# A limit of four weight loads in flight, and a first piece of split chunks, in an attention-then-experts kernel

## The chip, the cores and the metric

The kernel runs on one core of one Trainium2 chip. The metric is the device time of one execution in microseconds (us), the median of several runs. Times inside an execution are read from a hardware profile of one execution, and count from the start of its span.

## The reference

Attention over 8 batches of 12 heads (448 positions, head size 64, causal), whose output is the input of a layer of eight experts. Each token goes to the expert with its highest gate logit; each expert keeps the 80 tokens of highest gate weight; the rest of the output is zero.

```python
scores = scale * np.matmul(q, k.transpose(0, 1, 3, 2))
scores = np.where(mask, -1000000000.0, scores)
attn = np.exp(scores - np.max(scores, axis=-1, keepdims=True))
attn = attn / (np.sum(attn, axis=-1, keepdims=True) + 1e-09)
x = np.matmul(attn, v)                      # to 3584 tokens x 768
...
logits = x @ w_gate                         # 768 x 8
expert_idx = np.argmax(logits, axis=1)
for e in range(E):                          # 8 experts, capacity 80
    ...
    h = np.maximum(x[tok_idx] @ w1[e], 0.0)              # 768 x 1024
    out[tok_idx] = gate_w[tok_idx, None] * (h @ w2[e])   # 1024 x 768
```

## The kernel before, in words

The attention stage comes first, then a short stage that chooses the tokens of each expert, then the experts. The change touches the experts alone, from about 327 us on.

**Chunks and pieces.** A layer of an expert is a matrix `w1[e]` or `w2[e]`, cut into chunks of 128 rows: six chunks of 128x1024 for layer 1, eight of 128x768 for layer 2. A buffer named `wraw` is 3072 columns wide and holds one *piece*: three chunks of layer 1 or four of layer 2. There are 11 such buffers, filled before the expert stage begins with the first 11 entries of the list `PIECES`; the other 21 pieces (74 chunks, one DMA for each) are loaded during the stage by SP's queue, 0.38 MB or 0.5 MB a load, into buffers that have come free.

**What is done with a chunk.** Most chunks are *split*: ScalarE (ACT) makes the f16 high part `wh` (`high`, L1203), VectorE (DVE) the f16 low part `wl` (`low`, L1209), and TensorE (PE) multiplies three times in f16 for each block of 128 columns (L1504 to L1506). A split chunk's part of the buffer is free once its `wl` is made. Seven chunks are *whole*: PE multiplies them in f32 straight from `wraw` (L1501), and their part is free only when that product is done. The order of a layer's products stands in `ORDER`; where a layer has a whole chunk, that comes first (5, 0, 1, 2, 3, 4 for the first layer). Three half layers (`SOONER`) were split long before.

**What sets the order.** `plan_experts` plays through the stage with a table of costs and returns one list of turns: loads (`ld`), splits (`hi`, `lo`), products (`p`), the small steps between layers, and for each load which buffer takes it. The loop at the end of the kernel emits the instructions in that order. Each engine then runs its own instructions in order, and semaphores hold back what isn't ready. There are 12 `wh` and 11 `wl` buffers, so ACT and DVE can be that many chunks ahead of PE.

**How loads wait.** SP issues its DMAs in order. Their landings are told by eight semaphores (DMAHW0 to DMAHW7), which are dealt out in turn. So a load that takes a semaphore again waits until the DMA eight places ahead has landed, and also until the part of the buffer that it overwrites is free.

In `split_ahead`, buffers 3 and 4 are filled with the two pieces of layer 1 of expert 0: chunks 5, 0, 1 and chunks 2, 3, 4. Chunk 5 is a whole one.

Of the kernel before, what the change touches and what calls it, by code (L numbers as in the profile page):

```python
# [50 lines left out]
COST = {"hi1": 950, "hi2": 735, "lo1": 1135, "lo2": 870, "xw": 210, "xh": 460, "xl": 575, "hw": 120, "hh": 330, "hl": 400,  # L51
        "yt": 470, "yo": 490, "xtp": 420, "ytp": 660, "warm": 600, "split": 108, "whole": 224, "ld": 460, "far": 2100, "seen": 100, "slack": 900}
BEGIN = {"ACT": 400, "SP": 1500, "DVE": 5900, "PE": 9400}
GATHERED, GATHERS = [9400, 12500, 14500], 6000


def plan_experts(E, layers, blocks, order, whole, early, pieces, loaded, buffers, his, los, ready_h, ready_l):
# [63 lines left out]
    queue["SP"] = []  # L121
    busy, times, ends, out, gathers = dict(BEGIN), set(BEGIN.values()), {}, [], len(GATHERED)

# [53 lines left out]
def attention_then_moe(  # L177
# [12 lines left out]
    nc = tc.nc  # L190
# [67 lines left out]
    OFF, at = {}, 0  # L258
# [48 lines left out]
    def whole(e, which, c):  # L307

        return c == (NC1, NC2)[which - 1] - 1 and ((e, which) in WHOLE if AHEAD else e < E - which % 2 - 1)
# [3 lines left out]
    ORDER, sooner, PIECES = {}, [], []  # L313
    for x, (e, which) in enumerate(LAYERS):
        cs = sorted(range((NC1, NC2)[which - 1]), key=lambda c: (not whole(e, which, c), c))
        k = (K1, K2)[which - 1]
        if x in AHEAD:
            sooner.append((e, which, cs[:k]))
            PIECES.append((e, which, cs[k:]))
            cs = [c for both in zip(cs[:k], cs[k:]) for c in both]  # L320
        else:
            PIECES += [(e, which, cs[i:i + k]) for i in range(0, len(cs), k)]
        ORDER[e, which] = cs
    SOONER = [(e, which, c) for e, which, cs in sooner for c in cs]
    PIECES = sooner + PIECES
# [17 lines left out]
    def chunk_of(t, k, j):  # L343
        return t[:, j * (PW // k):(j + 1) * (PW // k)]

    def load_chunk(t, e, which, cs, j, x=0, parts=1):
        w = PW // len(cs) // parts
        nc.sync.dma_start(chunk_of(t, len(cs), j)[:, x * w:(x + 1) * w],
                          (w1 if which == 1 else w2)[e, :, cs[j], x * w:(x + 1) * w])

    def load_piece():

# [8 lines left out]
    def split_ahead():  # L361

        if not AHEAD:
            return [], []
        made = [wpool.tile([P, PW], F32, name="wraw", tag="w", bufs=WBUF) for _ in range(WBUF)]
        stage = made[-1]
        loads, splits = [], []
        for m, (e, which, c) in enumerate(SOONER):
            i, j = place_of[e, which, c]
            w = PW // len(PIECES[i][2])  # L370
            raw = stage[:, m % K2 * D:m % K2 * D + w]
            both = chunk_of(made[i], len(PIECES[i][2]), j).bitcast(F16)
            hi, lo = hi_of[e, which, c], lo_of[e, which, c] = both[:, 0:w], both[:, w:2 * w]
            h = w // 2
            loads.append([lambda x=x, raw=raw, e=e, which=which, c=c, h=h: nc.sync.dma_start(
                raw[:, x * h:(x + 1) * h], (w1 if which == 1 else w2)[e, :, c, x * h:(x + 1) * h]) for x in range(2)])
            splits.append([lambda raw=raw: nc.gpsimd.tensor_scalar(raw, raw, SW, None, op0=ALU.mult),
                           lambda hi=hi, raw=raw: nc.gpsimd.tensor_copy(hi, raw)] + [
                lambda a=a, hi=hi, lo=lo, raw=raw, h=h: nc.gpsimd.tensor_tensor(
                    out=lo[:, a:a + h], in0=raw[:, a:a + h], in1=hi[:, a:a + h], op=ALU.subtract) for a in (0, h)])  # L380
        wload.extend(made)
        later = [[lambda t=made[i], p=PIECES[i], j=j, x=x: load_chunk(t, *p, j, x, 2) for j in range(len(PIECES[i][2]))
                  for x in range(2)] for i in range(len(AHEAD), WBUF)]
        loads.append(later.pop())
        parts.extend(f for fs in later for f in fs)
        return loads, splits

    def piece_parts():

        got = []  # L390
        k = len(PIECES[len(wload)][2])
        got.append(piece())
        return [lambda j=j, x=x: load_chunk(*got[0], j, x, 2) for j in range(k) for x in range(2)]
# [806 lines left out]
    def high(y):  # L1200
        src = source(y)
        hi_of[y] = split_bufs["hi"].pop(0)
        nc.scalar.activation(hi_of[y][:, 0:src.shape[1]], src, AF.Copy, scale=SW)  # L1203

    def low(y):
        src = source(y)
        lo_of[y] = split_bufs["lo"].pop(0)
        n = src.shape[1]
        nc.vector.scalar_tensor_tensor(out=lo_of[y][:, 0:n], in0=src, scalar=SW, in1=hi_of[y][:, 0:n], op0=ALU.mult,  # L1209
                                       op1=ALU.subtract)  # L1210
# [160 lines left out]
    for i, x in enumerate(ROW_ENGINES):  # L1371
        g, t = divmod(i, NT)
# [38 lines left out]
    def gather(u):  # L1411
        e, s = u.e, u.s
        sn = min(SL, CAP - s * SL)
        u.sn = sn
        u.rows = max(2, sn)
        u.xg = xg_bufs[e % len(xg_bufs)]
        nc.gpsimd.indirect_dma_start(
            out=u.xg[0:u.rows, :], out_offset=None, in_=xs[:, :],
            in_offset=bass.IndirectOffsetOnAxis(ap=idx[s][0:u.rows, e:e + 1], axis=0),
            bounds_check=N - 1, oob_is_err=False)  # L1420
# [133 lines left out]
    for s in range(NSL):  # L1554
        units = [Unit(e, s) for e in range(E)]
        if s:
            for made in (raw_of, hi_of, lo_of):
                made.clear()
            del wload[BUFS:]
        turns = plan_experts(E, LAYERS, (None, NF, NC1), ORDER, whole, [] if s else SOONER, PIECES, 0 if s else BUFS, BUFS, HIS, LOS,  # L1560
                             0 if s else 3, 0 if s else 2)
        bufs = wload[0:BUFS]
        for u in units[:len(GATHERED)]:
            gather(u)
            if u.e == 0:
                nc.gpsimd.memset(split_bufs["lo"][0][:, 0:1], 0.0)  # L1566
        token_weights[s]()
        gathered = len(GATHERED)
        for (kind, e, *y), info in turns:
            u = units[e]  # L1570
            if kind == "hi":
                high((e, *y))
            elif kind == "lo":
                low((e, *y))
            elif kind == "ld":
                b, i, j = info
                load_chunk(bufs[b], *PIECES[i], j)
                raw_of[(e, *y)] = chunk_of(bufs[b], len(PIECES[i][2]), j)
            elif kind == "p":
                (u.last_layer if e == E - 1 and y[0] == 2 else u.product)(*(y[1:] if e == E - 1 and y[0] == 2 else y))  # L1580
                if not whole(e, *y) and (s or (e, *y) not in SOONER):
                    split_bufs["hi"].append(hi_of[(e, *y)])
                    split_bufs["lo"].append(lo_of[(e, *y)])
            elif kind == "warm":
                if PER == NC1:
                    warm = ps_m.tile([P, PER * SL], F32, name="wp", tag="misc")
                    for _ in range(3):
                        nc.tensor.matmul(warm, identb, before[:, 0:PER * SL], start=True, stop=True)
            else:
                getattr(u, kind)()  # L1590
                if kind == "xtp" and gathered < E:
                    gather(units[gathered])
                    gathered += 1
        units[-1].ytp()
        units[-1].yo()
# [44 lines left out]
```

## Time and profile before

| what | value |
|---|---|
| median of 3 runs | 446.72 us (446.46 to 448.32) |
| the profiled execution's own time | 446.64 us |
| its span | 444.6 us |
| PE busy, of the span | 419.5 us (94%) |
| DVE, ACT, POOL busy | 379.3, 388.3, 286.9 us |
| granted TensorE clock in every stretch of the expert stage | 1.00 |
| weight loads of the expert stage | 74, issued from 327.05 to 413.8 us |

The span is the time from the first to the last instruction of the profile; 2.0 us of the execution's own time lie around it. Busy time is a mean over stages, so the expert stage has to be read by itself. PE's matmuls and weight loads into the array (PEld) are separate instructions of one sequence.

### The profile page before, as it was taken

The page shows a single profiled execution, that of the slowest core. Times are in us where ns is not written, and L with a number is a line of the kernel's source. Part 1 is how long each engine was busy: PE and PEld are TensorE (multiplying, and loading weights), DVE is VectorE, ACT ScalarE, POOL GpSimd, SP SyncE. Part 2 cuts the span into 40 slices and gives each one's busy share as a digit, 9 for nine tenths or more (in the row PEclk, how much of TensorE's full clock was granted, in tenths as well). Part 3 has the DMA queues.
Part 4 walks back from the last instruction along what each step waited for, and adds up shares of the span by engine and source line. Part 5 has one row for each costly group of instructions (what it writes and reads, how often), then busy time and mean ns, then how long its engine had stood idle before and what let it go on. Part 6 is the DMA issues. An engine that isn't in the chain of part 4 may idle for free.

```text
span 444.6 us, 15877 instructions
## 1 busy us (share of the span) xinstructions
PE 419.5 (94%) x5847; PEld 325.2 (73%) x5847; DVE 379.3 (85%) x1302; ACT 388.3 (87%) x1062; POOL 286.9 (65%) x439
## 2 busy tenths in 40 slices
PE   7899999999999999999999999999789999888894
PEld 3666777677777777767777777766469999887893
DVE  6777788979889898988998989888879999989791
ACT  5899999999989999998999998978868979878891
POOL 7967998998898898899889885412462242210021
PEclk9899999999999999999999999999999999999999
DMA  7485668859786974976664387199359999999701
GB/s 224 147 272 184 195 227 285 291 201 295 241 282 199 290 242 152 297 253 212 214 215 144 124 243 272 66 349 312 126 171 349 403 403 411 393 414 413 306 27 46
DMA packets 49869, 109.95 MB, mean 247 GB/s; under 512 B 5970, under 2 KB 27474, under 8 KB 49152
## 3 DMA queue, kind: packets, MB, share of 16 engines
q1 hardware_dynamic: 48592, 105.20, 68.4%
q0 software_dynamic: 1056, 3.51, 2.4%
q8 instruction: 46, 0.75, 0.7%
q14 instruction: 31, 0.25, 0.2%
q10 hardware_dynamic: 144, 0.23, 0.2%
HBM read 85.35 MB, written 23.99 MB: 246 GB/s over the span
## 4 chain that ended last, share of the span: by engine, by line
PE 83%; ACT 5%; DVE 4%; issue 3%; POOL 2%; DMA 1%; POOLq 0%; DVEq 0%; ACTq 0%
PE xp L662 18%; PE tp L638 17%; PE sp L580 12%; PE rt L773 4%; ACT prob L603 4%; PE hp L1505 3%; PE hp L1506 3%; PE hp L1504 3%; PE op L1504 3%; PE op L1506 3%; PE op L1505 3%; PE gp L723 3%; PE sp L587 2%; PE hp L1501 2%; PE wp L1370 1%
## 5 line engine op out<-in xcount | busy, mean ns | idle before, releaser
L603 ACT ACTIVATE prob<-ns,nb 128x192 f32<-128x192 f32 (+3 forms) x336 | 175.5, 532 | 14.6 <-DVE nb L599 13.1
L599 DVE CUSTOM_DVE_ANT_0 ns<-sp,mask 128x192 f32<-128x192 f32 (+3 forms) x336 | 134.5, 443 | 17.7 <-PE sp L580 16.5
L638 PE MATMUL tp<-ident,prob 128*128 128x128 f32 x768 | 105.9, 279 | 0.1
L528 POOL TENSOR_TENSOR qk<-qk,qk 128x448 f16<-128x448 f32 x94 | 98.1, 1059 | 4.5 <-DVE qk L556 2.3
L1209 DVE SCALAR_TENSOR_TENSOR wl<-wraw,wh 128x768 f16<-128x768 f32 (+1 forms) x93 | 94.7, 1073 | 5.5 <-POOL wl L1566 2.1
L662 PE MATMUL xp<-PT,vt 128*64 128x448 f32 (+3 forms) x768 | 93.6, 386 | 0.2
L1203 ACT ACTIVATE wh<-wraw 128x768 f16<-128x768 f32 (+1 forms) x93 | 82.1, 941 | 12.3 <-PE hp L1505 5.9
L638 PEld LDWEIGHTS tp<-ident,prob 128*128 128x128 f32 x768 | 85.2, 142 | 3.2 <-ACT PT L643 0.5
L643 ACT COPY PT<-tp 128x512 f32<-128x512 f32 x144 | 77.0, 589 | 8.3 <-PE tp L638 7.0
L662 PEld LDWEIGHTS xp<-PT,vt 128*64 128x64 f32 x768 | 50.9, 136 | 44.7 <-issue 23.3
L580 PE MATMUL sp<-qk 64*128 64x448 f16 (+2 forms) x864 | 68.4, 297 | 2.9 <-POOL qk L528 1.8
L1506 PEld LDWEIGHTS <-wl 128*128 128x128 f16 x644 | 64.3, 100 | 3.9 <-issue 3.9
L603 ACT ACTIVATION_READ_ACCUMULATOR prob<-ns,nb 128x1 f32 x336 | 66.3, 197 | 0.0
L1504 PEld LDWEIGHTS <-wh 128*128 128x128 f16 x644 | 64.6, 100 | 1.7 <-issue 1.6
L1505 PEld LDWEIGHTS <-wh 128*128 128x128 f16 x644 | 64.3, 100 | 0.9 <-issue 0.8
L1550 POOL DMA_INDIRECT out<-yo,idx x8 | 15.6, 1954 | 69.4 <-ACT yo L1547 65.0
L580 PEld LDWEIGHTS <-qk 64*128 64x128 f16 x864 | 36.5, 94 | 17.7 <-issue 2.9
L643 DVE COPY PT<-tp 64x256 f32<-64x256 f32 x144 | 43.6, 328 | 2.9 <-PE tp L638 0.8
L1505 PE MATMUL hp<-xl,wh 128*128 128x80 f16 x344 | 38.8, 202 | 2.1 <-DVE xl L1449 1.2
L1506 PE MATMUL hp<-xh,wl 128*128 128x80 f16 x344 | 38.8, 202 | 1.1 <-issue 1.1
L1504 PE MATMUL hp<-xh,wh 128*128 128x80 f16 x344 | 38.9, 202 | 0.0
L556 POOL CAST qk<-qk 128x896 f16<-128x896 f32 x40 | 36.2, 935 | 0.4
(198 smaller groups left out, 734.7 us busy)
## 6 DMA issues: line engine op xcount, KB each, us to landing
wraw<-w SPq DMA_DIRECT2D x45, 384.0 KB
wraw<-w SPq DMA_DIRECT2D x31, 512.0 KB
out<-mask SPq DMA_DIRECT2D x56, 192.0 KB
qk<-k_t SPq DMA_DIRECT2D x23, 448.0 KB
qk<-q_t SPq DMA_DIRECT2D x23, 448.0 KB
vt<-v_t SPq DMA_DIRECT2D x24, 384.0 KB
xs<-xr SPq DMA_DIRECT2D x42, 192.0 KB
wraw<-w SPq DMA_DIRECT2D x24, 192.0 KB
```

Of the source, the lines that this page charges most:

```text
L528: sub = lambda e, o, a, b: e.tensor_tensor(out=o, in0=a, in1=b, op=ALU.subtract)
L580: nc.tensor.matmul(pr.sp[t, j], a[rows, p, queries(t)], c[rows, p, FROM[t]:FROM[t] + WIDTH[t]], start=(x == 0), stop=(x == 2))
L599: nc.vector.tensor_tensor_reduce(out=ns, in0=pr.sp[x], in1=m, scale=-1.0 / 8.0, scalar=HUGE, op0=ALU.add, op1=ALU.min, accum_out=nb)
L603: nc.scalar.activation(pr.P[:, OFF[x]:OFF[x] + w], got[0], AF.Exp, bias=got[1], scale=-1.0, accum_out=pr.sums[:, h:h + 1])
L638: nc.tensor.transpose(tp[:, i * P:(i + 1) * P], f, ident)
L643: way(part_of(pr.PT, rows, to, *todims), part_of(got[0], rows, at, *dims))
L662: nc.tensor.matmul(xp[rows, to:to + w], st["vt"][:, c, p * P + j * DH:p * P + (j + 1) * DH], pr.PT[:, j, n0:n0 + w], start=(c == 0), stop= ...
L1203: nc.scalar.activation(hi_of[y][:, 0:src.shape[1]], src, AF.Copy, scale=SW)
L1209: nc.vector.scalar_tensor_tensor(out=lo_of[y][:, 0:n], in0=src, scalar=SW, in1=hi_of[y][:, 0:n], op0=ALU.mult, op1=ALU.subtract)
L1504: nc.tensor.matmul(o, wh[:, ws], h[:, c, :], start=begin, stop=False, skip_group_check=True)
L1505: nc.tensor.matmul(o, wh[:, ws], l[:, c, :], start=False, stop=False, skip_group_check=True)
L1506: nc.tensor.matmul(o, wl[:, ws], h[:, c, :], start=False, stop=end, skip_group_check=True)
```

## The change

Two edits. The list `began` keeps the loads in order, and each load from the fifth on gets a wait for the landing of the load four places ahead of it. And the first ordinary layer of the list (layer 1 of expert 0) is cut into pieces in the order of the chunks' numbers, so that buffer 3 holds chunks 0, 1, 2, all of them split, and buffer 4 holds chunks 3, 4, 5. `ORDER`, which sets PE's products, stays.

```diff
+IN_FLIGHT = 4
...
         else:
-            PIECES += [(e, which, cs[i:i + k]) for i in range(0, len(cs), k)]
+            at = cs if PIECES else sorted(cs)
+            PIECES += [(e, which, at[i:i + k]) for i in range(0, len(cs), k)]
         ORDER[e, which] = cs
...
-        nc.sync.dma_start(chunk_of(t, len(cs), j)[:, x * w:(x + 1) * w],
-                          (w1 if which == 1 else w2)[e, :, cs[j], x * w:(x + 1) * w])
+        return nc.sync.dma_start(chunk_of(t, len(cs), j)[:, x * w:(x + 1) * w],
+                                 (w1 if which == 1 else w2)[e, :, cs[j], x * w:(x + 1) * w])
...
+        began = []
         for (kind, e, *y), info in turns:
...
             elif kind == "ld":
                 b, i, j = info
-                load_chunk(bufs[b], *PIECES[i], j)
+                began.append(load_chunk(bufs[b], *PIECES[i], j).ins)
+                if len(began) > IN_FLIGHT:
+                    tc.add_manual_dep(began[-1], began[-1 - IN_FLIGHT].name,
+                                      mybir.DependencyInfo(mybir.DependencyClass.Sync, mybir.DependencyReason.DATA),
+                                      reason="weights in flight")
```

On PE, ACT, DVE and POOL no instruction changes its place; only buffer numbers change. On SP the 74 loads keep their order of chunks; their buffers and waits change.

SP's queue at the start of the expert stage, before: the last write of the token rows (`xs`), then the first nine loads. `wraw_188` is buffer 4 (chunks 2, 3, 4 of expert 0), `wraw_187` is buffer 3 (chunks 5, 0, 1), `wraw_5724` is buffer 6.

```order
L798 DMA xs<-xrl_6563 128x384 [waits DMAHW3_49,Pool_49]
L348 DMA wraw_188<-w2 128x768 [waits DMAHW4_49,DVE_49]
L348 DMA wraw_188<-w2 128x768 [waits DMAHW5_49,DVE_49]
L348 DMA wraw_188<-w2 128x768 [waits DMAHW6_49,DVE_49]
L348 DMA wraw_188<-w2 128x768 [waits DMAHW7_49]
L348 DMA wraw_187<-w1 128x1024 [waits DMAHW0_49,PE_49]
L348 DMA wraw_187<-w1 128x1024 [waits DMAHW1_49]
L348 DMA wraw_187<-w1 128x1024 [waits DMAHW2_49]
L348 DMA wraw_5724<-w1 128x1024 [waits DMAHW3_49,DVE_49,Activation_49]
L348 DMA wraw_5724<-w1 128x1024 [waits DMAHW4_49,DVE_49,Activation_49]
```

The same place on SP in the changed kernel, where `wraw_187` now holds chunks 0, 1, 2 and `wraw_188` chunks 3, 4, 5.

```order
L800 DMA xs<-xrl_6563 128x384 [waits DMAHW3_49,Pool_49]
L350 DMA wraw_187<-w2 128x768 [waits DMAHW4_49,DVE_49]
L350 DMA wraw_187<-w2 128x768 [waits DMAHW5_49,DVE_49]
L350 DMA wraw_187<-w2 128x768 [waits DMAHW6_49,DVE_49]
L350 DMA wraw_187<-w2 128x768 [waits DMAHW7_49]
L350 DMA wraw_188<-w1 128x1024 [waits DMAHW4_49,DMAHW0_49,DVE_49]
L350 DMA wraw_188<-w1 128x1024 [waits DMAHW5_49,DMAHW1_49,DVE_49]
L350 DMA wraw_188<-w1 128x1024 [waits DMAHW6_49,DMAHW2_49,PE_49]
L350 DMA wraw_5724<-w1 128x1024 [waits DMAHW3_49,DMAHW7_49,DVE_49,Activation_49]
L350 DMA wraw_5724<-w1 128x1024 [waits DMAHW0_49,DVE_49,Activation_49]
```

The first four loads go to the buffer of chunks 0, 1, 2, whose `wl` of chunks 0 and 1 are made before the stage. The wait for PE (the product of the whole chunk 5) moves from the fifth load to the seventh. From the fifth load on, the semaphore of the load four places ahead is waited for, and from the ninth on it stands in place of the load's own.

SP's queue in the middle of the stage, before: six loads of layer 1 of expert 5 and two of layer 2 of expert 4.

```order
L348 DMA wraw_188<-w1 128x1024 [waits DMAHW0_49,DVE_49,Activation_49]
L348 DMA wraw_188<-w1 128x1024 [waits DMAHW1_49,DVE_49,Activation_49]
L348 DMA wraw_188<-w1 128x1024 [waits DMAHW2_49,DVE_49,Activation_49]
L348 DMA wraw_5724<-w1 128x1024 [waits DMAHW3_49,DVE_49]
L348 DMA wraw_5724<-w1 128x1024 [waits DMAHW4_49,DVE_49]
```

The same five in the changed kernel.

```order
L350 DMA wraw_187<-w1 128x1024 [waits DMAHW4_49,DVE_49,Activation_49]
L350 DMA wraw_187<-w1 128x1024 [waits DMAHW5_49,DVE_49,Activation_49]
L350 DMA wraw_187<-w1 128x1024 [waits DMAHW6_49,DVE_49,Activation_49]
L350 DMA wraw_5724<-w1 128x1024 [waits DMAHW7_49,DVE_49]
L350 DMA wraw_5724<-w1 128x1024 [waits DMAHW0_49,DVE_49]
```

Here only the semaphore differs: each waits for one that was dealt out four loads ago and not eight.

## Rows read from the trace of the kernel before

**Rows 1.** Windows: length, busy us (instructions) by engine, clock, DMA share, GB/s

```profile
331.00:336.00 5.00, 3.82 (x101) 3.82 (x101) 5.00 (x6) 2.94 (x5) 2.66 (x2) 1.00 1.00 331
344.00:349.00 5.00, 4.62 (x113) 4.49 (x112) 5.00 (x7) 4.67 (x9) 1.77 (x1) 1.00 1.03 411
349.00:384.00 35.00, 33.95 (x759) 33.58 (x756) 33.95 (x39) 31.29 (x47) 9.20 (x6) 1.00 1.03 400
384.00:418.00 34.00, 28.08 (x718) 27.33 (x714) 28.45 (x33) 27.00 (x39) 4.56 (x3) 1.00 1.03 414
418.00:422.00 4.00, 2.92 (x82) 2.79 (x79) 4.00 (x6) 4.00 (x9) 0.00 (x0) 1.00 0.40 157
422.00:434.60 12.60, 12.60 (x333) 12.58 (x330) 12.60 (x16) 11.57 (x19) 2.97 (x2) 1.00 0.09 24
```

**Rows 2.** Waits of PE from 348 to 422: us in total, times, longest

```profile
PE op L1506 <- issue: 3.0, 3, 1.0
PE op L1504 <- issue: 2.5, 3, 1.3
PE ytp L1537 <- issue: 1.1, 1, 1.1
PE hp L1506 <- issue: 1.1, 1, 1.1
PE hp L1505 <- issue: 0.7, 1, 0.7
```

**Rows 3.** Windows cut where PE's idle times end, columns as in the first group

```profile
385.60:391.59 5.99, 4.98 (x128) 4.84 (x127) 4.79 (x7) 3.19 (x5) 0.74 (x1) 1.00 1.02 416
391.59:397.51 5.92, 5.21 (x128) 5.06 (x128) 4.90 (x6) 5.38 (x8) 0.45 (x1) 1.00 1.03 415
...
415.33:421.38 6.05, 4.97 (x128) 4.84 (x127) 4.07 (x7) 4.65 (x9) 0.00 (x0) 1.00 0.72 285
421.38:426.40 5.02, 5.00 (x128) 5.00 (x128) 5.02 (x7) 5.02 (x9) 1.60 (x1) 1.00 0.02 5
426.40:430.99 4.59, 4.59 (x134) 4.59 (x131) 4.59 (x7) 4.59 (x7) 1.26 (x1) 1.00 0.20 57
```

**Rows 4.** DMA from 391.59 to 397.51: packets, MB, share; issues, us to landing

```profile
q8 instruction: 1, 0.02, 1.0%
...
out<-yo,idx POOLq DMA_INDIRECT x1, 6.8
```

**Rows 5.** The same from 430.99 to 436

```profile
q8 instruction: 1, 0.02, 1.2%
...
out<-yo,idx POOLq DMA_INDIRECT x1, 4.2
```

**Rows 6.** Waits of SP's queue from 327 to 414

```profile
SPq L348 <- DMA wraw<-w: 48.8, 60, 1.7
SPq L348 <- DVE wl L1209: 10.5, 13, 5.1
```

**Rows 7.** Timeline of SP: start, us, instruction

```profile
321.32 0.55 SPq L798 DMA_DIRECT2D xs<-xrl  x1
327.05 87.30 SPq L348 DMA_DIRECT2D wraw<-w  x74
```

**Rows 8.** Timeline of DVE from 415 to 438, in brackets the idle time before

```profile
417.33 0.66 DVE L1449 SCALAR_TENSOR_TENSOR xl<-xtp,xh 128x480 f16<-128x480 f32 x1 [1.98 <-ACT xh L1443]
...
427.58 7.03 DVE L1209 SCALAR_TENSOR_TENSOR wl<-wraw,wh 128x768 f16<-128x768 f32 x8
```

**Rows 9.** The chain that ended last, the step after PE's last product

```profile
437.37 0.42 DVE yt L1523
```

**Rows 10.** Timeline of ACT, its last split

```profile
432.01 0.84 ACT L1203 ACTIVATE wh<-wraw 128x768 f16<-128x768 f32 x1
```

**Rows 11.** Timelines of POOL and PE as the stage begins

```profile
324.56 1.08 POOL L1417 DMA_INDIRECT xg<-xs,idx  x1 [5.16 <-DVE gws L1134]
...
322.68 5.46 PE L1370 MATMUL wp<-before,identb 128*128 128x448 bf16 x28
```

## The prediction

> **What bounds the kernel now.** The page says PE is busy for 94% of the span, but that is a mean. The change touches only the expert stage, so I read the stage by windows first [rows 1]. Up to 384 us PE is nearly full (33.95 of 35.00 us). From 384 to 418 it is idle for 34.00 - 28.08 = 5.9 us, from 418 to 422 for 1.1, and after that not at all. The DMA share changes at the same place: 1.03 up to 418, 0.40 in the next four microseconds, 0.09 after them. The granted clock is 1.00 throughout, so the clock has no part in it.
>
> The waits of PE come next [rows 2]. There are nine from 348 to 422, of about a microsecond each, 8.4 us in all, and none is for a buffer, a split or a load: they stand as "issue", so nothing that the profile shows was missing.
>
> Then I cut windows where these idle times end [rows 3]. Each of them holds 128 matmuls and 127 or 128 weight loads: 256 instructions. That regular count is the key. A wait for data would follow layers and chunks; this one comes after every 256th instruction, whatever it is. In two windows of one block each, one with loads and one without (it follows the last of these rows), the queue of kind "instruction" moved one packet of 0.02 MB [rows 4, 5]. So I read the idle time as PE waiting for its next block of instructions, fetched by DMA once a block. While weights stream, a block takes 5.92 to 6.05 us, of which PE works 4.97 to 5.21; as soon as they end, a block of as many instructions takes 5.02 or 4.59 us with no idle time [rows 3]. The fetch, some 5.95 us from block to block, is slower than the work by 0.8 to 1.1 us, and only beside the loads.
>
> One rule speaks against this. The Trainium skill ("Runtime: NRT & Kernel Launch", section "Instruction fetch mechanics") says that instructions come in blocks of 256 over a queue of the engine's own, and that the crossing of a block is mostly hidden. The count of 256 agrees with the trace, the hiding does not: by the page there would be nothing to win, by the rows there are 8.4 us.
>
> **The change part by part.** *The limit of four.* SP's queue waited 60 times for the landing of an earlier load, 48.8 us in all [rows 6]: eight loads were in flight nearly always. The 74 issues take 87.30 us [rows 7], 1.18 each, so a load is issued about 9.4 us after the one eight places ahead, and 4.7 us after the one four ahead. The change therefore takes about 4.7 us of queued weights from in front of whatever else wants the DMA engines. The fetch has to become quicker by 0.8 to 1.1 us for the stalls to go, a fifth of that. How the fetch's wait hangs on the queue no row shows. Its bounds are: no gain at all (0) and all of it (8.4). The nearest rows are those of a scatter, a DMA on another queue too: it landed in 6.8 us beside the loads and in 4.2 without them [rows 4, 5], 2.6 more. Half of that is 1.3, more than the 1.1 that is needed, so I take all of the 8.4 as the likeliest.
>
> *What comes of the 8.4 us.* PE does not keep them all, since DVE is close behind. DVE has no idle time from 417.33 on: it is full in 418 to 422 and in 422 to 434.60 [rows 1], and its last `wl` ends at 427.58 + 7.03 = 434.6 [rows 8]. That run began after 1.98 us of waiting for `xh` of the last expert, which follows PE's transposes, and so PE's stalls. Before it DVE was idle for 34.00 - 28.45 = 5.55 us in the window from 384, the 1.98 among them [rows 1]. If PE loses its stalls, DVE can move up by 5.55 us and no further (another 1.05 us of idle time lies before 384). At the end PE finishes by 437.37 [rows 9], 2.8 us after the last `wl`. In PE's order (`last_layer`) 36 of the 54 matmuls of the last three chunks follow that `wl`: the last chunk's part of the first half, then the whole second half. At 4.59 us for 134 or 5.02 for 128 [rows 3] that is 1.2 to 1.4 us. So the tail can give another 1.4. Together 5.55 + 1.4 = 6.95 us, less than the 8.4. I take 6.0: the waits of DVE for `xh` need PE, ACT and DVE in a row, and I expect about a microsecond of them to stay.
>
> *The price of the limit.* Nothing but loads stands behind the waiting load on SP, so the wait itself holds up no other work. It can only make the weights late. They have room: the last `wh` is made at 432.01 [rows 10], while the last load is issued at about 414 [rows 7] and the DMA share falls between 418 and 422 [rows 1]; I take 421 for its landing. That is 11 us, and 5 us once the stage is 6 us shorter. From 344 on the DMA moved 411 x 5 + 400 x 35 + 414 x 34 + 157 x 4 = 30.8 MB in 77 us [rows 1]. To be done by 426 it needs 376 GB/s, 9% less than 414. The bounds of the rate with four loads: 414, as now, and 331, that of 331 to 336 [rows 1], soon after the first loads began. There the share was 1.00 already, and gathers of token rows ran beside the loads, which is why I take a value near the upper end: a loss of at most a few per cent, which the 11 us hide.
>
> *The first piece.* SP had issued its last row write at 321.32 and was free at 321.87, then waited 5.1 us, its longest wait for DVE, for the first load's part of the buffer [rows 6, 7]. The first two loads now go where `wl` was made before the stage, so they start at about 322, 5 us sooner: 0.79 MB, 1.9 us of transfer at 414 GB/s, off the end of the stream. It is more room, not time, as loads were not waited for. A cost could come from a meeting with the first gather (issued at 324.56), on which PE's first transposes wait; but the two loads need until about 322 + 1.9 and some issue time, and PE is filled by 28 warm-up matmuls to 322.68 + 5.46 = 328.1 anyway [rows 11]. If that cover failed, the stage would begin later by what is left of the two loads, at most 1.9 us. I count 0.
>
> *Sum.* 446.64 (the execution's own time) - 6.0 = 440.6; the median of the runs lies 0.08 above that execution, so 440.7.
>
> **The rivals.** *Half.* The fetch gets quicker, but by half of what is needed. Then 4.2 us of stalls stay, DVE's limit no longer counts, and the time is 446.7 - 4.2 = 442.5, or up to 444.5 where less than half goes. For it: blocks vary from 4.59 to 5.21 us of work, so some may fit and others not.
>
> *The fetch takes turns.* If the fetch's wait is set by how the engines serve several queues and not by how much is queued on one, a shorter queue changes nothing. For it: the scatter landed only 2.6 us later beside the loads [rows 4, 5], though some 9 us of them were queued: it did not stand behind all of them. Against it: all rows are of eight in flight, so none shows the wait at another depth. The stalls would stay, and the time would be 446.7, give or take 1. The Trainium skill ("DMA: Bandwidth & Descriptors", section "Queues, rings and completion order") states such a rule: each DMA engine goes round the queues that have work, a packet at a time. The scatter's row bears it out in part.
>
> *Weights come late.* With four in flight the engines run dry between a landing and the next issue. At 331 GB/s the 30.8 MB would take 93 us, to 437.1, 5.1 us after the last `wh` was made before; the end moves with it, to 446.6 + 5.1 = 451.7. It decides from about 350 GB/s down: there the last landing is at 432 and the gain is gone. Against it: a load has 4.7 us from the issue four places ahead, and share 1.00 was reached early in the stage [rows 1].
>
> **How the numbers follow.** The forecast has 0.62 (439.0 to 442.2 by itself: the DVE sum of 6.95 with some of the 1.05, down to 4.5), half 0.14, turns 0.13, late weights 0.11. A difference within 0.5% (2.2 us) can hardly be told from none here. Faster is the forecast and most of half, 0.74; the same is turns and the rest, 0.15; slower 0.11. The range reaches from 438.6, where nearly all of the 8.4 us are kept, to 446.0, so that it leaves out late weights and much of turns.
>
> **What would show it.** Right: PE's waits marked "issue" between 348 and 422 fall from 8.4 us to under 2, windows of 128 matmuls last about 5 us under load, SP's waits for landings remain, and the DMA rate stays above 376 GB/s. DVE should be nearly full from 384 on. Wrong: the stalls still stand at every 256th instruction (turns), or ACT's `wh` and PE's whole products wait for `wraw` (late weights). If the first step holds and the time still does not fall, DVE's order was tighter than I summed.

## The result, and the profile after

The change made the kernel slower: 452.48 us (median of 4 runs, 450.1 to 453.55) against 446.85 us (4 runs, 446.46 to 448.32), a ratio of 1.0112 with a 95% interval of 1.0066 to 1.0159. The prediction was 440.7 (438.6 to 446.0). The profiled execution took 452.68 us, with a span of 450.8, 6.2 us more than before.

The windows of the changed kernel, columns as in [rows 1], and two more at the end:

```profile
331.00:336.00 5.00, 5.00 (x124) 5.00 (x123) 5.00 (x6) 3.47 (x6) 2.52 (x2) 1.00 1.02 323
344.00:349.00 5.00, 5.00 (x135) 5.00 (x131) 5.00 (x7) 4.67 (x10) 2.16 (x1) 1.00 0.95 303
349.00:384.00 35.00, 33.03 (x732) 32.69 (x732) 33.30 (x37) 29.91 (x45) 13.31 (x5) 1.00 0.97 326
384.00:418.00 34.00, 29.17 (x738) 28.38 (x738) 27.93 (x30) 27.38 (x38) 2.61 (x3) 1.00 0.96 344
418.00:422.00 4.00, 3.29 (x76) 3.09 (x76) 3.80 (x6) 4.00 (x8) 0.00 (x0) 1.00 0.95 334
422.00:434.60 12.60, 9.81 (x256) 9.40 (x254) 11.32 (x15) 9.77 (x15) 0.92 (x1) 0.99 0.98 339
434.60:440.00 5.40, 3.15 (x34) 2.97 (x35) 2.77 (x3) 3.19 (x5) 0.76 (x1) 0.50 0.03 13
440.00:451.00 11.00, 4.41 (x90) 3.89 (x87) 1.02 (x2) 0.95 (x2) 1.07 (x2) 0.81 0.16 46
```

Read the last column first. The DMA moved 326 to 344 GB/s from 349 to 434.6, where it moved 400 to 414 before [rows 1], and the weights, which were all there by 422, now come until 434.6. Read the share beside it: 0.95 to 0.98, near the 1.03 of before. The share alone would not have told that the rate had fallen by a sixth.

The waits of PE from 348 to 451 (us in total, times, longest), which answer to [rows 2]:

```profile
PE ytp L1539 <- ACT yt L1530: 4.5, 1, 4.5
PE hp L1506 <- ACT xh L1445: 2.2, 2, 1.6
PE op L1508 <- issue: 1.8, 2, 1.1
PE op L1506 <- issue: 1.8, 1, 1.8
PE hp L1507 <- DVE xl L1451: 1.0, 2, 0.5
PE op L1508 <- DVE wl L1211: 0.5, 1, 0.5
PE hp L1507 <- issue: 0.4, 2, 0.3
PE ytp L1539 <- DVE yt L1525: 0.2, 1, 0.2
```

What was meant to fall has fallen: "issue" is 1.8 + 1.8 + 0.4 = 4.0 us, from 8.4. But 8.4 us of waits for ACT and DVE stand here, of which before had only the 0.2 at the bottom. So I look at what ACT waits for, from 327 to 440:

```profile
ACT wh L1205 <- DMA wraw<-w: 8.1, 11, 1.3
```

Eleven splits waited for their weights, 8.1 us in all; before there was no such wait. ACT works in order, so what stands behind a late split is late too. At the end of the stage this can be followed, on ACT's timeline (start, us, instruction, in brackets the idle time before and what ended it):

```profile
432.68 1.79 ACT L1205 ACTIVATE wh<-wraw 128x768 f16<-128x768 f32 x2 [1.24 <-DMA wraw<-w]
435.50 0.84 ACT L1205 ACTIVATE wh<-wraw 128x768 f16<-128x768 f32 x1 [1.03 <-DVE wl L1211]
436.24 0.55 ACT L1530 ACTIVATE yt<-op 128x480 f32<-128x480 f32 x1
436.69 0.83 ACT L1205 ACTIVATE wh<-wraw 128x768 f16<-128x768 f32 x1
```

and on PE's and DVE's:

```profile
436.85 1.50 PE L1539 MATMUL ytp<-ident,yt 128*80 128x128 f32 x6 [4.53 <-ACT yt L1530]
```

```profile
437.56 0.96 DVE L1211 SCALAR_TENSOR_TENSOR wl<-wraw,wh 128x768 f16<-128x768 f32 x1 [0.23 <-ACT wh L1205]
443.59 0.41 DVE L1525 TENSOR_SCALAR yt<-hp 128x240 f32<-128x240 f32 x1 [5.07 <-PE hp L1508]
```

`yt` stands in ACT's order behind the late splits, and PE stood 4.53 us for it. The last split began at 436.69, 4.7 us later than before [rows 10], and PE's last product ended by 443.59, 6.2 us later [rows 9]: the whole difference of the spans. The other 1.5 us lie behind that split. There PE had much of its tail still to do, and until 440 it did it at a granted clock of 0.50, that is 1.2 GHz, to which the clock had fallen while PE was without work. How the 1.5 us divide between the two was not measured.

SP's timeline, and from the DMA view of 349 to 418 the loads of which issue and landing could be paired (count, KB each, median us from one to the other):

```profile
321.30 109.59 SPq L350 DMA_DIRECT2D wraw<-w  x74
```

```profile
DMA packets 7109, 23.09 MB, mean 335 GB/s; under 512 B 902, under 2 KB 902, under 8 KB 7094
...
q1 hardware_dynamic: 6583, 21.12, 88.1%
...
wraw<-w SPq DMA_DIRECT2D x24, 512.0 KB, 6.2
wraw<-w SPq DMA_DIRECT2D x22, 384.0 KB, 5.5
```

The first load starts at 321.30 and not at 327.05 [rows 7], as said. But the 74 issues take 109.59 us, so four of them 5.92, and a load needs 5.5 to 6.2 us from issue to landing. I had put 4.7 there, half of the 9.4 us of eight loads.

### The profile page after: what moved, and what is told of

It reads as the page before. It is cut to its first block, busy times and chain, and to the rows that moved or that the text cites. A ratio compares the mean times of both kernels' runs of the same rounds, so it can differ in the third digit from the quotient of the medians.

```text
span 450.8 us, 15879 instructions
## 1 busy us (share of the span) xinstructions
PE 421.4 (93%) x5847; PEld 326.2 (72%) x5847; DVE 379.7 (84%) x1302; ACT 389.1 (86%) x1062; POOL 287.8 (64%) x439
## 4 chain that ended last, share of the span: by engine, by line
PE 81%; DMA 7%; DVE 4%; ACT 3%; POOL 2%; issue 1%; POOLq 0%; ACTq 0%; SPq 0%; DVEq 0%
PE xp L664 19%; PE tp L640 18%; PE sp L582 13%; DMA wraw<-w 6%; PE rt L775 4%; PE gp L725 2%; PE hp L1507 2%; PE hp L1508 2%; PE hp L1506 2%; PE hp L1503 2%; PE sp L589 2%; PE op L1506 2%; PE op L1507 2%; PE op L1508 2%; PE wp L1372 2%
## 5 line engine op out<-in xcount | busy, mean ns | idle before, releaser
L640 PE MATMUL tp<-ident,prob 128*128 128x128 f32 x768 | 104.6, 276 | 0.1
L1205 ACT ACTIVATE wh<-wraw 128x768 f16<-128x768 f32 (+1 forms) x93 | 83.4, 942 | 19.1 <-DMA wraw<-w 8.1
L640 PEld LDWEIGHTS tp<-ident,prob 128*128 128x128 f32 x768 | 83.9, 141 | 3.2 <-ACT PT L645 0.5
L1507 PEld LDWEIGHTS <-wh 128*128 128x128 f16 x644 | 65.0, 101 | 2.9 <-issue 2.7
L1506 PEld LDWEIGHTS <-wh 128*128 128x128 f16 x644 | 65.3, 101 | 1.2 <-issue 1.2
```

The source lines that it names most:

```text
L640: nc.tensor.transpose(tp[:, i * P:(i + 1) * P], f, ident)
L1506: nc.tensor.matmul(o, wh[:, ws], h[:, c, :], start=begin, stop=False, skip_group_check=True)
L1507: nc.tensor.matmul(o, wh[:, ws], l[:, c, :], start=False, stop=False, skip_group_check=True)
```

## The experiments

The theory after the result: the limit does shorten PE's wait for the instruction fetch (for its next block of instructions), but with the bytes of four loads in flight the DMA moves only some 335 GB/s, and the weights end too late. Its rivals: the limit costs something by itself (the added waits, the order on SP); the new first piece is what costs; the stalls were not the loads' doing, so that there was nothing to win.

In one table, all kernels. GB/s are those of the windows 349 to 384 and 384 to 418; "issue" is PE's, from 348 to 422; "wraw" is ACT's wait for loads, from 327 to 440; the last column is how long SP takes to issue all loads. Kernels that ran together share the runs of before: 446.7 us for e1 to e4, 447.65 for e5 to e8, 446.86 for e9 to e11. All but before, e2 and e4 have the new first piece, so what a limit does by itself is read against e1. Times are medians, but each trace is of one execution: those of e3 (447.43 us) and e9 (443.40) were the longest of their kernel, that of e7 (442.36) the shortest.

| kernel | median us (runs) | ratio to before, 95% | GB/s | issue us | wraw us | issues us |
|---|---|---|---|---|---|---|
| before | 446.72 | | 400, 414 | 8.4 | 0 | 87.30 |
| the change | 452.48 (4) | 1.0112, 1.0066 to 1.0159 | 326, 344 | 4.0 | 8.1 | 109.59 |
| e1 first piece only | 445.11 (10) | 0.9969, 0.9952 to 0.9987 | 399, 403 | 6.6 | 0 | 89.77 |
| e2 limit only | 453.72 (4) | 1.0170, 1.0144 to 1.0195 | 338, 350 | 0.2 | 7.7 | 105.51 |
| e3 limit of six | 445.00 (10) | 0.9970, 0.9956 to 0.9984 | 379, 399 | 6.9 | 0 | 94.18 |
| e4 no loads | 437.23 (4) | 0.9791, 0.9760 to 0.9822 | 32, 25 | 0 | 0 | none |
| e5 limit of five | 444.20 (4) | 0.9915, 0.9898 to 0.9931 | 359, 374 | 5.4 | 0 | 100.13 |
| e6 halves by partitions | 482.08 (4) | 1.0765, 1.0747 to 1.0783 | 253, 260 | 10.1 | 17.5 | 141.81 (148 halves) |
| e7 four from the 41st load | 444.52 (5) | 0.9937, 0.9920 to 0.9953 | 382, 355 | 5.4 | 0 | 100.46 |
| e8 four from the 57th load | 443.26 (4) | 0.9895, 0.9875 to 0.9914 | 401, 371 | 4.9 | 0 | 96.45 |
| e9 four, every sixth load left out | 440.85 (4) | 0.9855, 0.9833 to 0.9877 | 321, 337 | 4.2 | 0 | 94.08 (62 loads) |
| e10 halves by columns | 451.65 (4) | 1.0120, 1.0089 to 1.0151 | 342, 346 | 1.7 | 4.3 | 107.92 (148 halves) |
| e11 five, four from the 57th | 444.01 (4) | 0.9926, 0.9909 to 0.9944 | 375, 375 | 5.6 | 0 | 100.96 |

**e1 and e2: each edit alone.** e1 keeps the new first piece and lifts the limit out of reach; e2 keeps the limit and cuts the first piece as before.

```diff
 e1
-IN_FLIGHT = 4
+IN_FLIGHT = 1000
 e2
-            at = cs if PIECES else sorted(cs)
+            at = cs
```

> The first piece of split chunks alone, no limit on loads in flight. If the limit is what costs (the queue of loads too short, weights late): 446 to 447 us, PE's waits marked issue stay near 8.4 us, and the DMA rate from 349 to 418 stays near 400 to 414 GB/s. If the two early loads are what costs, by meeting the first gather or by a slower start: 449 to 452 us, with the first product of the experts later than 329.0 us.

> The limit of four alone, the first piece as before. If the limit costs: 452 to 455 us, a rate near 330 to 345 GB/s from 349 on, ACT waiting about 8 us or more for loads, since the two early loads no longer take 0.79 MB off the stream. If the early loads cost: 446 to 447 us or faster.

The loss is the limit's: 453.72 without the new piece. The new piece gains a little, 0.3%, some 1.4 us, where I had written 446 to 447. The window from 418 to 422 of e1 shows where most of it stands:

```profile
418.00:422.00 4.00, 4.00 (x104) 3.99 (x102) 4.00 (x7) 4.00 (x7) 0.00 (x0) 1.00 0.07 25
```

The loads, begun earlier, are all but done by 418 (25 GB/s here, 157 before), and PE, which was idle for 1.1 us of this window, is full: the last stall of [rows 2], 1.1 us, is gone with the load traffic beside it. In this trace PE's last product ends 1.8 us sooner than before, and most of the other 0.7 lies in two stalls before 361 us that were shorter.

In e2 PE's waits are these, from 348 to 422:

```profile
PE hp L1506 <- ACT xh L1445: 3.9, 3, 1.8
PE hp L1507 <- DVE xl L1451: 1.5, 3, 0.5
PE ytp L1539 <- ACT yt L1530: 1.1, 1, 1.1
PE op L1506 <- issue: 0.2, 1, 0.2
```

Almost no "issue" is left, and yet the kernel is the slowest of those with whole loads. I read it so: an engine that waits for data gives the fetch time to arrive. Then the 0.2 us here are not what the limit would leave of the stalls with the weights in time; e9, which has them in time, has 4.2.

**e4: no loads.** The 74 loads of the expert stage are left out, with the first piece as before; the experts compute with what the buffers hold.

```diff
-                began.append(load_chunk(bufs[b], *PIECES[i], j).ins)
-                if len(began) > IN_FLIGHT:
...
```

> The 74 loads of the expert stage are left out: the products use what the buffers held before, the rest of the work stays. If the stalls at every 256th instruction come from the loads: no wait of PE marked issue over 0.3 us, and the time falls by what I summed, 6 to 7 us, to 439.7 to 441 us. If they are the fetch's own, beside loads or not: stalls stay near 8 us and the time near 446.7.

From 348 to 422 PE has no wait at all, and these are two windows:

```profile
349.00:384.00 35.00, 35.00 (x802) 34.97 (x799) 35.00 (x40) 32.87 (x50) 16.90 (x6) 1.00 0.12 32
384.00:418.00 34.00, 34.00 (x897) 33.97 (x894) 34.00 (x41) 33.12 (x50) 15.22 (x4) 1.00 0.09 25
```

The stalls are the loads' doing, and taking the loads away is worth 446.7 - 437.2 = 9.5 us. That is more than the 8.4 of the stalls, and more than the 6.95 that I took to be the most that DVE allows. (I had written 439.7 to 441.)

That the stalls are waits for the fetch can be read from the single packets in the traces. Every wait marked "issue" of over 0.2 us that PE has from 348 us on, in every kernel, ends at the same place of a block: at instruction 193 of 256, counting PE's matmuls and weight loads from the start. In the kernel before, the 16 KB packet of the queue of kind "instruction" starts 3.5 to 4.0 us after PE has passed such a place (349 to 418 us, mean 3.7), and in its nine stalls PE goes on 2.2 to 2.5 us after that start. Together that is the 5.95 us from block to block. Without loads the packet starts 0.2 us after the place in the mean, 1.3 at most.

**e9: four in flight, fewer bytes.** This tells the late weights from a cost of the limit itself. The limit and its waits stay, but every sixth load is left out, so that the stream is shorter; those chunks are computed from what the buffer held.

```diff
-                began.append(load_chunk(bufs[b], *PIECES[i], j).ins)
+                turned += 1
+                if turned % 6 != 0:
+                    began.append(load_chunk(bufs[b], *PIECES[i], j).ins)
```

> The changed kernel with the limit of four, but every sixth weight load of the expert stage is left out (62 of the 74 remain, each of its full size), so that chunk is computed from what the buffer held before. Late weights: the rate with four in flight stays at 325 to 350 GB/s, but the stream has 16% fewer bytes and ends near 418 instead of 436, before any split waits for it; ACT's waits for wraw go to under 1 us, PE's waits for instructions stay at about 4 us, and the time is 440 to 443 us. The limit costs by itself (the wait on SP's queue, or something else than bytes): the time stays at 449 us or more, although fewer bytes are loaded.

The windows around the end of the stream, and PE's waits from 348 to 422:

```profile
384.00:418.00 34.00, 29.98 (x771) 29.37 (x771) 31.05 (x36) 29.62 (x45) 4.52 (x3) 1.00 0.95 337
418.00:422.00 4.00, 4.00 (x103) 3.99 (x102) 4.00 (x6) 4.00 (x8) 0.51 (x1) 1.00 0.44 169
```

```profile
PE op L1506 <- issue: 1.4, 1, 1.4
PE ytp L1539 <- issue: 1.1, 1, 1.1
PE hp L1508 <- issue: 0.8, 1, 0.8
PE op L1508 <- issue: 0.7, 1, 0.7
PE op L1507 <- issue: 0.2, 1, 0.2
```

The rate is as low as in the changed kernel (337 GB/s), the loads end between 418 and 422, no split waits for one, and the time is 440.85, 6.0 us under before. No cost of the limit but the late weights is seen here. And with the weights in time 4.2 us of stalls stay, of 8.4 before and of 6.6 in e1, which has the first piece alone: the fetch is quicker, but by less than was needed. (The profiled execution, with 443.4 us, was the longest of the four.)

**e10 and e6: what sets the rate.** Each load is made as two DMAs, with at most eight of them in flight: the bytes of four loads, in twice as many transfers. e10 halves the columns, e6 the partitions (two DMAs of 64 partitions each).

```diff
 e10
-                began.append(load_chunk(bufs[b], *PIECES[i], j).ins)
+                for x in range(2):
+                    began.append(load_chunk(bufs[b], *PIECES[i], j, x, 2).ins)
 e6
+                for rows in (slice(0, P // 2), slice(P // 2, P)):
+                    began.append(nc.sync.dma_start(chunk_of(bufs[b], len(pcs), j)[rows],
+                                                   (w1 if pw == 1 else w2)[pe, rows, pcs[j], :]).ins)
```

> Each weight load is made as two DMAs of half its columns, all 128 partitions each, with at most eight halves in flight: the bytes of four loads. Bytes in flight set the rate: 325 to 350 GB/s from 349 to 418, ACT's waits for wraw at 7 us or more, and 449 to 454 us. The number of transfers in flight sets it: 390 to 415 GB/s, as with eight whole loads, waits for wraw under 1 us, and a time at or under that of the kernel before, 443 to 447 us. If the halves are slower to move by themselves, as the halves by partitions were, the rate falls under 325 GB/s and the time passes 455 us.

> Each load cut into two DMAs of 64 partitions, eight halves in flight: as many bytes in flight as four loads, released in finer steps, and packets of the same size. If the bytes in flight set the rate: 335 to 355 GB/s and 450 to 453 us. If it is the wait for a whole load, whose last DMA engine ends some 2 us after its first, the rate rises to 370 GB/s or more and the time falls to 447 us or less.

e10 moves 342 and 346 GB/s, the changed kernel 326 and 344, and takes about as long. Twice as many transfers do not bring the rate back: the bytes in flight set it. One rival is that e10's packets are half as large. They are a little slower for their size: from 349 to 418 the median packet of 2048 B took 84 ns, against 159 ns for 4096 B in the changed kernel, and one of 1536 B took 65 ns, against 121 for 3072 B. These 6 to 7% are too little for 342 in place of 400. ACT's wait was less than I had written, 4.3 us for at least 7. e6, for which I had written 450 to 453 us or less, tells nothing on this, since its halves are slower by themselves: the median packet of 3072 B took 194 ns there. Its windows:

```profile
349.00:384.00 35.00, 30.36 (x615) 29.78 (x613) 25.84 (x31) 24.06 (x36) 5.00 (x5) 0.90 1.04 253
384.00:418.00 34.00, 26.20 (x559) 25.45 (x556) 20.69 (x23) 21.15 (x29) 2.67 (x3) 0.90 1.02 260
```

But it repeats the lesson on the share: 1.04 and 1.02 at 253 and 260 GB/s. The Trainium skill ("SBUF — State Buffer", section "Door 1: The DMA port swizzle (why `[64,N]` ≈ `[32,N]`)") says that 64 partitions reach only 8 of the 16 ports of the memory, and gives 196 GB/s for such a transfer of 1 MiB against 328 for 128 partitions; the fall agrees in kind, and no run here shows the ports.

**e3 and e5: six and five in flight.**

```diff
-IN_FLIGHT = 4
+IN_FLIGHT = 6    (e3)
+IN_FLIGHT = 5    (e5)
```

> Both edits with six loads in flight in place of four. If the rate is set by how much is in flight, six loads (2.6 MB) that land in some 6 us should be near 400 GB/s again, and the weights come in time: then the time tells whether the fetch of instructions gets quicker already. 442 to 445 us if PE's stalls fall to 4 us or less, 446 to 447 if they stay at 8.4. If every load less in flight costs rate (six eighths of 414 is 310): 453 us or more.

> Both edits with five loads in flight. Seen so far from 384 to 418: 344 GB/s at four, 399 at six, 403 to 414 without a limit. If the rate grows with what is in flight: 365 to 380 GB/s, the last landing near 427, and the time between those of six and four, 445 to 448 us. If PE's stalls begin to fall at five already (under 5 us) while the weights still come in time: 441 to 444.

The rate rises with each load in flight (326, 359, 379, 399 GB/s for 4, 5, 6 and 8 from 349 to 384), and the stalls with it: 5.8 us at five and 8.0 at six, with the 0.4 and 1.1 us that lie just behind 422, since the loads end later there. That six has more than the 6.6 of e1, without a limit, shows how far single traces differ. At five nothing waits for a load yet, and the kernel is 0.85% faster than before. The limit of six gains nothing: e3 is as fast as e1.

**e7, e8 and e11: the limit where there is room.** A lower rate costs nothing as long as the weights are ahead. e7 keeps the limit of four from the 41st load on, e8 from the 57th; e11 has five in flight and four from the 57th.

```diff
-                if len(began) > IN_FLIGHT:
+                if len(began) > 40:         (e7)
+                if len(began) > 56:         (e8)
 e11
+                far = 4 if len(began) > 56 else 5
+                if len(began) > far:
```

> First piece of split chunks, and the limit of four only from the 41st load on. Those 34 loads are about 14 MB: at 340 GB/s in place of 405 they take some 41 us, not 35, so the last lands near 426. If the limit is good for the fetch and bad only for the rate, PE's stalls from 384 on fall from 7 us to about 2 to 4 and the weights are just in time: 441 to 444 us. If the fetch does not get quicker at four: 445 us. If the weights are late after all: 446 to 449.

> The same with the limit of four only from the 57th load on, 18 loads, about 7.3 MB: 3.4 us more, the last landing near 423. Stalls of PE after about 397 us (some 5 us of the 8) can shrink, the earlier ones stay: 442 to 444 us if the fetch gets quicker, 445 if not. Weights should not be late in any case.

> The limit is five up to the 56th load of the expert stage and four from the 57th on. If the gain of the limit of five (0.9915 of before) and that of the late limit of four (0.9895) come from different blocks, they add up in part: 441 to 443 us, PE's waits for instructions 4 us or less from 348 to 422. If the rate of five in flight (359 GB/s from 349 to 384) uses up the room that the late limit needs, the last loads come late: ACT waits for wraw for 2 us or more, and the time is 444 to 448 us.

All three beat both kernels. e8 is the best, 443.26 us, 1.05% under before, some 0.7% of it more than e1; its interval meets that of e5. e7, with 444.52, is hardly to be told from e1, whose interval it meets. In e11 the two limits did not add up to the 441 to 443 us of my first case: 444.01, with 5.6 us of "issue", and no split waits for a load, so late weights are not why. Which of its blocks miss the fetch was not followed further.

## Why the prediction was wrong

**The step that failed: the price of the limit.** I took the rate with four loads "near the upper end: a loss of at most a few per cent, which the 11 us hide". It was 335 GB/s (349 to 418), below the 376 that I had said was needed and close to my lower bound of 331. The rival *weights come late* came true: it gave 451.7, and 452.48 was measured. That it came so near is in part luck. The loads had begun earlier, so that their last packet ended at 435.9 and not at 437.1, and the 1.5 us behind the last split, which the rival did not count, made up for it. Two readings led to the wrong price.

The first is the sentence against that rival, "a load has 4.7 us from the issue four places ahead". Halving the queue does not halve the time to a landing. Per group of loads in flight, SP's issues take 89.77 x 8 / 74 = 9.70 us for eight (e1), 7.64 for six, 6.77 for five, 5.92 for four. From eight to four that is 3.78 us, 0.95 a load, so some 5.92 - 4 x 0.95 = 2.1 us of a group don't shrink (an estimate, by a straight line; SP's waits for free buffers are in these times too). The Trainium skill ("DMA: Bandwidth & Descriptors", section "Anatomy of one DMA — SWDGE (gpsimd) path") has such a part: about 2.0 us of each DMA that do not depend on its size, most of it until the last byte is confirmed, and 436 GB/s besides. Its figures are for DMAs issued from another engine; by them four loads of 0.461 MB (the mean of the 46 above) would land in 2.0 + 4 x 0.461 / 0.436 = 6.2 us, an estimate that is near the 5.5 to 6.2 of the trace.

The second is the share of 1.00 beside 331 GB/s in [rows 1], which I read as a full DMA held up by gathers. The share does not tell full from half-idle: it was 0.97 at 326 and 1.04 at 253 GB/s. What it counts is the time that packets take, and that grows in the mean. From 349 to 418 the loads' queue had 6583 packets in 88.1% of 16 engines' 69 us, 148 ns each, and before:

```profile
DMA packets 8932, 28.06 MB, mean 407 GB/s; under 512 B 1103, under 2 KB 1103, under 8 KB 8918
...
q1 hardware_dynamic: 8406, 26.10, 95.2%
```

that is 125 ns each. The usual packet is not slower: the median is 121 ns for 3072 B and 159 ns for 4096 B in both traces. But 8% of the packets took more than one and a half times the median of their size, against 1.2% before; why these take longer stays open. And the engines do run dry in part, as the rival put it: for 38% of these 69 us fewer than 16 packets were under way on the 16 engines, before never. The share does not show it, since the records of some packets overlap.

**The stalls.** Right in kind, wrong in size. They belong to the loads (e4: none without them) and the limit shortens them, but I took all 8.4 us where 4.2 go (e9), and 1.8 of these by the first piece (e1). That is the rival *half*, which gave 442.5; e9, with no late weights, took 440.85. *The fetch takes turns* is wrong as an all or nothing, but the wait is not in proportion to the queue either. From the place of the block to the start of the fetch's packet it took, in the mean from 349 to 418, 3.7 us at eight (before) or 3.5 (e1), 3.5 at six, 3.3 at five, 3.2, 2.8 and 2.6 at four (the changed kernel, e9, e2) and 0.2 without loads. I had taken 1.3 us off, half of what the scatter lost beside the loads; 0.8 to 1.1 were needed, and the mean of e9 is 0.9 below before. So some blocks fit and others don't. A low rate alone does not shorten the wait: in e6, at 253 GB/s, its mean is 4.1.

**What comes of them.** The bound of 6.95 us by DVE was too low: without loads the kernel gained 9.5 us, with DVE full from 349 to 418. I had counted DVE's idle time from 384 on and 1.4 us of tail. DVE's timeline in e4 shows which term was wrong:

```profile
419.51 7.03 DVE L1211 SCALAR_TENSOR_TENSOR wl<-wraw,wh 128x768 f16<-128x768 f32 x8
428.02 0.41 DVE L1525 TENSOR_SCALAR yt<-hp 128x240 f32<-128x240 f32 x1 [1.49 <-PE hp L1508]
```

The tail behind the last `wl` gave 1.3 us (1.49 in place of 2.76), as summed. But the last `wl` ends at 426.54, 8.1 us sooner and not 5.55: the 1.05 us of idle time before 384, which I had left out, went as well. Where the other 1.5 was to be found was not followed further.

**The first piece.** Its loads started 5.75 us earlier, at 321.30, and PE went from the warm-ups to the first transposes without a wait, so the first gather did not suffer. (The transposes began at 328.85, 0.9 us later than before, since the warm-ups took longer; the last section has their clock.) I counted 0; by itself it gains 0.3% (e1), in the main because the loads are gone from beside the last stall. With the limit it cannot be told from nothing (1.0112 and 1.0170, whose intervals meet).

**The room.** The 11 us fit what came: the loads ended some 14 us later than the 421 that I had read (their last 0.29 MB came after 434), and that is more than the room. The engines' order made it worse: `yt` waits on ACT behind a split, and PE behind `yt`.

## What to carry to other kernels

Before a limit is put on transfers in flight, work out the bytes in flight over the time from issue to landing, with a part of it that does not shrink, and compare that rate with what the stage needs; a high DMA share said nothing here about the rate. A queue that is too deep for its neighbours is best cut where the transfers are ahead of their users: with the new first piece, the same limit of four is 1.1% slower than before over the whole stage and 1.05% faster on its last 18 loads, of which the first piece alone gives 0.3%. And a wait that shrinks after a change may only be covered by a new one: read it in a run where the new one cannot occur.

## What the runs showed of the hardware

- The rate of weight loads of 0.39 and 0.52 MB hangs on the bytes in flight: from 349 to 384 us 326 GB/s with four, 359 with five, 379 with six, 399 with eight; eight halves by columns, the bytes of four, gave 342.
- The DMA share stayed between 0.95 and 1.04 while the rate went from 414 down to 253 GB/s.
- A load as two DMAs of 64 partitions each fell to 253 to 260 GB/s, as two of half the columns it did not.
- PE passed the end of a block of 256 instructions, and the packet that fetches the next one started 3.5 to 4.0 us later beside eight loads in flight, 0.2 us later in the mean without loads; PE could go on 2.2 to 2.5 us after that start. Work of 4.6 to 5.2 us a block did not cover this beside eight loads.
- The granted TensorE clock was 0.50 (1.2 GHz) from 321.60 to 325 in the warm-up of the changed kernel, and 1.00 at the same place of before. The 28 warm-up matmuls took 6.88 us, and 5.46 before [rows 11]. It does not follow the change: e1, which has the new first piece, did not show it, and e4, which has the first piece of before and no loads, did. Nor do I see it in what PE did just ahead: it was busy for 2.29 us of the 3.60 from 318 to 321.60, in e1 for 2.39, in e4 for 2.39 too. The windows and the timeline of the changed kernel:

```profile
318.00:321.60 3.60, 2.29 (x26) 1.14 (x24) 3.32 (x14) 3.57 (x9) 0.74 (x1) 1.00 0.40 128
321.60:325.00 3.40, 3.15 (x12) 1.46 (x13) 0.94 (x6) 3.40 (x5) 1.08 (x2) 0.50 0.88 273
```

```profile
322.14 6.88 PE L1372 MATMUL wp<-before,identb 128*128 128x448 bf16 x28
```
